# Linear-attention heads feeding a convolution-gated FFN on one core: attention regrouped into one visit per group on four 64x64 tiles, FFN output products one unit late

## The chip, the core and the metric

The kernel runs on one core of one Trainium2 chip. The metric is the device time of one execution in microseconds (us). The kernel before took 343.77 us, the median of three runs (343.47 to 345.69). The changed kernel computes the same thing from the same inputs.

## What is computed

Four batches of eight heads, sequence 768, head width 48. Each head carries a 48x48 state that decays by a vector `w` per step; the output of all heads, 384 wide, goes through a gated FFN of width 1024.

```python
for t in range(S):                       # B=4, H=8, S=768, D=48
    cur = einsum('bhd,bhe->bhde', u * k[t], v[t])
    y[t] = einsum('bhd,bhde->bhe', r[t], state + cur)
    state = w[:, None] * state + einsum('bhd,bhe->bhde', k[t], v[t])
x = y as (B, S, 384)
h = relu(x @ w_in)                       # 384 -> 1024
c = sum_k conv_w[k] * h[t + k - 1]       # 3 taps along the sequence
out = (h * sigmoid(c)) @ w_out           # 1024 -> 384
```

The 768 steps of a batch are cut into six groups of 128 steps, each of two chunks of 64. Inside a chunk the recurrence becomes matrix products: scores (k against r, masked), the diagonal term with `u`, the state's contribution, and the update of the state. `w`'s powers scale k and r beforehand so that the decay is folded in.

## The kernel before

**Order.** Nothing is scheduled at run time. Every piece of work is recorded as an operation with the engines it may run on and a planned cost (`Plan.op`); `Plan.order` then writes one fixed order for each engine, choosing by due times that are counted back from the FFN products, corrected by the table `OFF`. Elementwise products marked "any" go to VectorE (DVE) or GpSimd (POOL), whichever the planner finds better. SyncE (SP) issues every DMA, in one fixed order too. An engine whose next instruction waits holds up everything behind it.

**Attention.** A group's k and r arrive transposed (`KR`, head dimension on the partitions) and token-wise (`KT`), v in `WW`; three buffers of each (`NBUF`). `prep` scales k and r by powers of `w` on DVE (line 351, `KR<-KR,TKR`), moves the scaled r by DMA into the operand tiles `RA` and `RB` (rows 48 wide that share a tile with the masked scores), scales the token-wise k and moves it by DMA into `KTA` and `KTB`, and writes the diagonal into `RA`/`RB` with two selects on POOL (line 566). `scores` is 16 float32 products (lines 581, 582) on two quarters of the array, followed by two masked copies on DVE (line 592). `step` is, for each chunk, 8 products that make the next state (lines 604, 605; the decay is a diagonal block `KTd` beneath k, so 112 or 128 rows deep) and two copies of it on ScalarE (ACT) back into `WW` (line 611), and 8 products that make the output (lines 618, 619). So there are 48 products to a group, in four separate stretches on TensorE (PE). `yout` copies the output to `YY` on ACT (line 628); when two groups are there, six small DMAs `YY<-YY` spread the eighth head pair over the others' free partitions, and then `XT`, the FFN's operand, is written as a high and a low float32r half (line 639 on ACT, line 351).

**FFN.** A unit is a batch's third (batch 0: 254, 256, 258 columns) or half (384 columns); there are nine. For each of a unit's eight blocks of 128 FFN channels, `first` is 9 products into one of two PSUM banks `HP` (line 680), then ReLU on ACT in place (684), middle tap on ACT (685), two taps on DVE (688), sigmoid on ACT (691), the gate product on DVE (692), and the high (ACT, 694) and low half (`GL`, "any", 351). The bank is free only when the gate product has read it. `second` is 9 products of that block into three banks `PO` (line 709), three blocks later (`LAG = 3`). The weights arrive as 64-bit words and are converted on ACT, DVE and "any" (lines 482 to 492). Until the FFN's output products begin, small bf16 products on zeros (line 764) fill gaps of PE.

Of the kernel before, what the change touches and what calls it, by code (L numbers as in the profile page):

```python
# [13 lines left out]

DR = 2
DK = 8
DS = 24
DQ = 6
VIS = 4
SLACK = -8.0  # L20
VWAIT = 0.3
ALONE, AFTER = (), 0
POOLED = ()
LAG = 3
WPRE = 2
LEAD = 6
UP = '3sss'
SPLIT = 2
NW = 12
NT = 3  # L30
T0 = 20
SLOW = 0
TS = 40
DELTA = 0.1
OFF = {
    "ST": -1.69, "f2": -4.55, "T2": 1.29, "X": -1.7, "GL": 0.45, "wi": 5.15, "GG": 11.38, "TT": 4.36,
    "KR": -3.61, "kmv": 0.76, "GH": 0.48, "wo": 1.32, "Rs": -0.21, "av": -1.42, "SG": 3.12, "T1": -2.33,
    "rmv": -12.84, "ymv": -0.78, "wlo": 0.9, "sc": -6.54, "S": 0.59, "ldK": 0.4, "ldT": -0.2, "ldV": -0.95,
    "TK1": -4.02, "TH0": -2.43, "uu": 1.28, "Rz": -2.77, "PW2": -3.54, "o2": 0.26, "cw": -1.69, "KTd": -3.79,
    "psY": -8.17,  # L40
}
PB = 2
ZD = 0
FILL = True
FG = 0
FE = 5000
FN = 256
FW = 3.4
BON = 6
NST = 3  # L50
NBUF = 3

# [9 lines left out]
U = 386  # L62
PAT = {"2": [(0, 382), (382, 386)], "s": [(0, 384), (384, 384)], "3": [(0, 254), (254, 256), (510, 258)]}
UNITS = [(b,) + x for b in range(B) for x in PAT[UP[b]]]
NU = len(UNITS)
WS = 256.0


class Plan:
# [6 lines left out]
    def __init__(self):  # L76
        self.ops = []
        self.last_w, self.last_r = {}, {}
        self.port = []
        self.visits, self.visit, self.rank = {}, {}, {}  # L80

    def op(self, eng, dur, rd, wr, fn, cls="", x=0.0, port=False, visit=None):

# [18 lines left out]
        self.ops.append((dur, x, sorted(pred), fn, cls))  # L105
        self.port.append(port)
        if visit is not None:
            self.visits.setdefault(visit[0], []).append(n)
            self.visit[n], self.rank[n] = visit
        return n  # L110

    def late(self):
# [3 lines left out]
        for i, (dur, x, pred, fn, cls) in enumerate(ops):  # L116
            if "pe" in dur and x:
                late[i] = t
                t += dur["pe"] * (1 + (SLOW if t < TS else 0.0))
# [5 lines left out]
        for i in range(n):  # L125
            late[i] -= OFF.get(ops[i][4], 0.0)
        for m in self.visits.values():
            t = min(late[k] for k in m)
            for k, i in enumerate(sorted(m, key=self.rank.get)):
                late[i] = t + 1e-3 * k  # L130
        return late

    def order(self):
# [3 lines left out]
        left = [0] * n  # L137
        for i in range(n):
            left[i] = len(ops[i][2])
            for j in ops[i][2]:  # L140
                succ[j].append(i)
# [10 lines left out]
        fill, hist = FILL, []  # L152
        lanes = [0.0] * 7
        mode, cur, slack = 0, None, SLACK
        todo_v = {v: set(m) for v, m in self.visits.items()}
        ext = {}
        for v, m in self.visits.items():
            inner = set(m)
            for i in range(n):
                if any(j in inner for j in ops[i][2]) and any(i in ops[k][2] for k in m):  # L160
                    inner.add(i)
            ext[v] = {j for k in m for j in ops[k][2]} - inner
        end_of = [None] * n
        todo = n
        while todo:
            best = None
            for e in self.ENG:
                av = avail[e]
                if not av:
                    continue  # L170
                f = free[e]
                if e == "pe":
                    if cur is not None:
                        av = [i for i in av if self.visit.get(i) == cur]
                    else:
                        c = []
                        for i in av:
# [121 lines left out]
def rwkv_ffn_kernel(tc, krd, krt, vt, wd, ut, w_in, conv_w, w_out, out):  # L299
# [4 lines left out]
    with ExitStack() as ctx:  # L304
# [318 lines left out]
        def yout(g):  # L623
# [6 lines left out]
            if k == 0:  # L630
                return
# [196 lines left out]
```

## Time and profile before

| | |
|---|---|
| timed runs | 343.77 us median (343.47, 343.77, 345.69) |
| span of the profiled execution, first to last instruction | 349.2 us |
| median of the runs against that span | 5.4 us shorter |
| mean granted PE clock | 0.954 |
| busy, of the span | PE 91%, DVE 72%, ACT 62%, POOL 54% |
| bytes moved by DMA | 44.41 MB |

The profile is of one execution; the page gives its span, and no time of its own beyond that. Idle time of an engine is put down to whatever ended it. Records of PE show two for each float32 product (two passes) and one for each float32r product; PEld is the loading of weights, which overlaps.

### The profile page before, as it was taken

How to read it: one execution, taken by the hardware profiler on the slowest of the kernel's cores; microseconds unless marked ns; L12 is line 12 of the kernel's file. 1: busy time of each engine (PE TensorE's matmuls, PEld its weight loads, DVE VectorE, ACT ScalarE, POOL GpSimd, SP SyncE). 2: the span in 40 equal slices, each digit the busy share in tenths (PEclk: the TensorE clock that was granted, in tenths of full speed). 3: DMA queues.
4: the chain of work that ended last, by engine and by line, in shares of the span. 5: the costliest groups of instructions: out<-in, count | busy, mean ns of one | idle time of the engine just before them, and what ended most of it. 6: DMA issues, size and time to landing. Idle time of an engine off the chain costs nothing.

```text
span 349.2 us, 9698 instructions
## 1 busy us (share of the span) xinstructions
PE 319.1 (91%) x3838; PEld 296.3 (85%) x3838; DVE 252.4 (72%) x412; ACT 215.2 (62%) x513; POOL 188.1 (54%) x214
## 2 busy tenths in 40 slices
PE   8899877989998898889869989999899999999995
PEld 4678767879887897879869979999899999999995
DVE  6966868789896788697597797775675655665560
ACT  4516669677756674564547555775575856766751
POOL 8847978688989685956743540232332221242230
PEclk9759989699999999999969999999999999999999
DMA  7958698424564759686624730235420200200101
GB/s 188 266 163 238 211 277 221 156 91 103 172 191 130 219 155 243 168 247 141 191 78 128 188 110 2 79 99 122 128 75 8 75 1 2 79 2 2 68 2 68
DMA packets 25117, 44.41 MB, mean 127 GB/s; under 512 B 5296, under 2 KB 15920, under 8 KB 25072
## 3 DMA queue, kind: packets, MB, share of 16 engines
q1 hardware_dynamic: 25072, 43.79, 45.2%
q8 instruction: 30, 0.49, 0.6%
q14 instruction: 15, 0.12, 0.1%
HBM read 30.40 MB, written 4.72 MB: 101 GB/s over the span
## 4 chain that ended last, share of the span: by engine, by line
PE 52%; DMA 18%; DVE 10%; ACT 8%; POOL 4%; SPq 3%; issue 3%; ACTq 0%; DVEq 0%; POOLq 0%
PE HP L680 22%; PE PO L709 17%; DMA KR<-in_krd_dram 11%; DMA KT<-in_krt_dram 4%; PE psC L581 4%; SPq L354 3%; PE psS L604 3%; PE psY L618 3%; DVE KR L351 2%; DVE CV L688 2%; ACT WW L611 2%; DMA uc<-in_ut_dram 2%; PE PO L764 2%; ACT SG L691 1%; DMA YY<-YY 1%
## 5 line engine op out<-in xcount | busy, mean ns | idle before, releaser
L680 PE MATMUL HP<-XT,wi 128*128 128x386 f32 (+3 forms) x648 | 120.7, 334 | 11.3 <-DVE SG L692 9.7
L680 PEld LDWEIGHTS HP<-XT,wi 128*128 128x128 f32 x648 | 107.1, 197 | 16.4 <-DVE SG L692 13.4
L709 PE MATMUL PO<-GH,wo 128*128 128x384 f32 (+3 forms) x432 | 111.0, 321 | 0.9 <-ACT OS L716 0.9
L688 DVE SCALAR_TENSOR_TENSOR CV<-HP,cw,CV 128x384 f32<-128x384 f32 (+3 forms) x144 | 81.1, 569 | 24.1 <-ACT CV L685 22.6
L351 POOL TENSOR_TENSOR GL<-SG,GH 128x384 fp32r<-128x384 f32 (+3 forms) x49 | 48.5, 990 | 85.4 <-ACT GH L694 71.1
L709 PEld LDWEIGHTS PO<-GH,wo 128*128 128x128 f32 x432 | 76.9, 190 | 1.6 <-ACT OS L716 1.3
L709 PE MATMUL PO<-GL,wo 128*128 128x384 f32 (+3 forms) x216 | 69.6, 322 | 1.2 <-DVE GL L351 1.2
L691 ACT ACTIVATE SG<-CV 128x384 f32<-128x384 f32 (+3 forms) x72 | 35.2, 489 | 36.8 <-DVE CV L688 36.2
L692 DVE TENSOR_TENSOR SG<-HP,SG 128x384 f32<-128x384 f32 (+3 forms) x72 | 36.6, 509 | 23.5 <-ACT SG L691 23.0
L684 ACT ACTIVATE HP<-HP 128x386 f32<-128x386 f32 (+3 forms) x72 | 31.8, 441 | 30.8 <-PE HP L680 30.0
L351 DVE TENSOR_TENSOR KR<-KR,TKR 112x1024 f32<-112x1024 f32 (+1 forms) x26 | 32.8, 1265 | 18.7 <-DMA KR<-in_krd_dram 14.9
L694 ACT CAST GH<-SG 128x384 fp32r<-128x384 f32 (+3 forms) x72 | 34.1, 474 | 18.8 <-DVE SG L692 18.5
L709 PEld LDWEIGHTS PO<-GL,wo 128*128 128x128 f32 x216 | 41.1, 190 | 1.6 <-DVE GL L351 1.4
L685 ACT ACTIVATE CV<-HP,cw 128x384 f32<-128x384 f32 (+3 forms) x72 | 39.2, 545 | 1.6
L611 ACT COPY WW<-psS 48x192 f32<-48x192 f32 x88 | 27.5, 313 | 15.1 <-PE psS L605 13.5
L604 PE MATMUL psS<-WW,KTA 112*48 112x48 f32 x352 | 26.0, 219 | 7.7 <-ACT WW L611 6.0
L604 PEld LDWEIGHTS psS<-WW,KTA 112*48 112x48 f32 x352 | 20.6, 130 | 13.5 <-ACT WW L611 7.1
L566 POOL TENSOR_SCALAR_AFFINE_SELECT RA<-QQ 64x512 f32<-64x512 f32 x24 | 20.3, 848 | 18.2 <-PE psY L619 17.1
L582 PE MATMUL psC<-KR 48*64 48x64 f32 x384 | 29.0, 229 | 0.0
L581 PE MATMUL psC<-KR 48*64 48x64 f32 x384 | 29.0, 229 | 0.0
L618 PE MATMUL psY<-RA,WW 112*48 112x64 f32 x384 | 27.6, 226 | 0.0
L619 PE MATMUL psY<-RB,WW 128*48 128x64 f32 x384 | 27.6, 226 | 0.0
(86 smaller groups left out, 512.3 us busy)
## 6 DMA issues: line engine op xcount, KB each, us to landing
KR<-in_krd_dram SPq DMA_DIRECT2D x24, 448.0 KB, 5.0
KT<-in_krt_dram SPq DMA_DIRECT2D x18, 384.0 KB, 4.3
WW<-in_vt_dram SPq DMA_DIRECT2D x48, 96.0 KB, 3.7
out_dram<-OS SPq DMA_DIRECT2D x18, 192.0 KB, 1.9
ST<-in_w_in_dram SPq DMA_DIRECT2D x8, 384.0 KB, 4.0
ST<-in_w_out_dram SPq DMA_DIRECT2D x8, 384.0 KB, 3.8
RA<-KR SPq DMA_DIRECT2D x22, 96.0 KB, 4.2
RB<-KR SPq DMA_DIRECT2D x22, 96.0 KB, 4.0
```

Source lines behind the costliest of these rows:

```text
L351: op(eng, d, rd, wr, lambda e: e.tensor_tensor(**kw), cls, port=True)
L581: PE.matmul(psC[0:64, n:n + C], kk[64:112, p, t], rr[64:112, p, t], start=True, stop=True)
L604: PE.matmul(psS[64:112, n:n + D], KTA[i][:, p, c, :], WA[i][:, p, c, :], start=True, stop=True)
L611: lambda e, T=T, ps=ps, o=o: A.copy(T[j][o:o + 48, :, cn, :], ps[o:o + 48, 0:NP * D].rearrange("q (p d) -> q p d", p=NP)))
L618: PE.matmul(psY[64:112, n:n + C], WA[i][:, p, c, :], RA[i][0:112, p, t], start=True, stop=True)
L680: PE.matmul(hp, wi[a][:, j, fs], X[:, x, j, t], start=(j == 0 and k == 0), stop=(j == 2 and k == 2))
L685: op("act", act(n) + 0.05, [H_, "cw"], [("T", ti)], lambda e: A.activation(t1, hp[:, 1:n + 1], AF.Copy, scale=cw[:, 3 * f + 1:3 * f + 2]), ...
L688: op("dve", dve(n + 60), [H_, "cw"], [("T", ti)], lambda e, k=k: V.scalar_tensor_tensor(out=t1, in0=hp[:, k:n + k], scalar=cw[:, 3 * f + k ...
L691: op("act", act(n), [("T", ti)], [("SG", ti)], lambda e: A.activation(sg, t1, AF.Sigmoid))
L692: op("dve", dve(n), [H_], [("SG", ti)], lambda e: V.tensor_tensor(out=sg, in0=hp[:, 1:n + 1], in1=sg, op=ALU.mult), "GG")
L694: op("act", act(n), [("SG", ti)], [("GH", gi)], lambda e: A.copy(gh, sg))
L709: PE.matmul(PO[m][:, :n], wo[a][:, f, ms], g2[x], start=(f == 0 and k == 0), stop=(f == NF - 1 and k == 2))
```

## The change

The planner's special rules for visits and the table `OFF` are gone (two entries stay), and its planned costs are other ones; with them, the fixed orders of all engines are new. What is computed in another way:

- `visit(g)` does all products of one step of the loop as one operation on PE: the outputs of group g together with the scores and state updates of group g+1, 64 float32 products, for each chunk and head pair eight of them on the four 64x64 quarters of the array: two scores, two state-times-r, two k-times-v, two outputs.
- The decay of the state is an elementwise product (`M`, any engine), followed by an addition from PSUM on DVE (`SA`). The diagonal blocks `KTd`, the copies of the state on ACT, and the operand tiles `RA`, `RB`, `KTA`, `KTB` are gone with their DMAs.
- The diagonal of the scores is written by an "any" product (`dg`), the mask by one copy of 128 partitions.
- The output goes from PSUM straight into `XT` as high (ACT) and low half (DVE); `XT` has a fourth block for the eighth head pair, which six DMAs a group spread. Before, they were six for two groups.
- `second` of a unit runs beside `first` of the next unit, block of output channels by block of output channels, into a single bank `PO`; there are 13 buffers of gated values instead of five, and four banks `HP` instead of two.
- Units are 254, 256, 258 for batch 0 and 382, 386 for the others; `w_out` is converted in six pieces instead of eight. The zero products end with the first FFN product.

```diff
-        HP = [pst.tile([128, 512], F32, name=f"HP{i}") for i in range(2)]
-        PO = [pst.tile([128, 512], F32, name=f"PO{i}") for i in range(NM)]
+        SP_ = pst.tile([128, NP, 2, C], F32, name="SP")
+        UP = pst.tile([128, 512], F32, name="UP")
+        AV = pst.tile([128, NP, 2, C], F32, name="AV")
+        HP = [pst.tile([128, 512], F32, name=f"HP{i}") for i in range(NH)]
+        PO = pst.tile([128, 512], F32, name="PO")
...
+        def visit(g, av, su):
...
+            def mm(e):
+                for c in range(2):
+                    for p in range(NP):
...
+                        for x in range(2):
+                            if su:
+                                PE.matmul(SP_[xs[x], p, c], KK[j][rows[x], p, t], RR[j][rows[x], p, t], start=True, stop=True)
+                        for x in range(2):
+                            if av and not (first and c == 0):
+                                PE.matmul(outs[x], state(2 * g + c)[rows[x], p], RR[i][rows[x], p, t], start=True, stop=False)
+                        for x in range(2):
+                            if su and not (c == 1 and gj == GPB - 1):
+                                n = (c * NP + p) * D
+                                PE.matmul(UP[rows[x], n:n + D], TOK[j][xs[x], 0, p, c], TOK[j][xs[x], 2, p, c], start=True, stop=True)
+                        for x in range(2):
+                            if av:
+                                PE.matmul(outs[x], TOK[i][xs[x], 2, p, c], SC[g % 2][xs[x], p, c], start=first and c == 0, stop=True)
...
+                op("dve", dve(512, psum=1), ["SUs", "mask"], [("SC", k)], lambda e: V.copy_predicated(
...
+                        tt("any", 192, [ka, "PW2"], [("M", c)], "M", out=m, in0=a, in1=w64, op=ALU.mult)
+                        tt("dve", 192, [("M", c), "SUu"], [kb], "SA", 1, out=b, in0=m, in1=u_, op=ALU.add)
...
+                op("act", act(512), ["AV"], [kh], lambda e: A.copy(xh, y), "XH")
+                tt("dve", 512, ["AV", kh], [kl], "XL", 1, out=xl, in0=y, in1=xh, op=ALU.subtract)
                 for o in (0, 64):
+                    for jx in range(3):
+                        dma([kh, kl], [("Xm", b % 2, gi, o, jx)], X[o + 48:o + 64, :, jx, t].bitcast(F32), X[o + 16 * jx:o + 16 * jx + 16, :, 3, t].bitcast(F32), 0.5, 0.08, "mv")
...
+        for u in range(NU + 1):
+            a, b = need(u), need(u + 1)
+            for f in range(NF):
+                if u:
+                    for k in range(3 * f, 3 * f + 3):
+                        second(u - 1, k)
+                if u < NU:
+                    first(u * NF + f)
```

How the fixed orders stand at three places. **PE, one group in the middle of the program**, before: `psS` takes the state, `psY` the outputs, `psC` the scores, and each stretch is of one kind.

```order
L709 MATMUL PO_126<-GH_97,wo_144 128x384
L604 MATMUL psS<-WW_78,KTA_72 48x48
L605 MATMUL psS<-WW_78,KTB_75 48x48
...
L618 MATMUL psY<-RA_63,WW_78 48x64
L619 MATMUL psY<-RB_66,WW_78 48x64
...
L581 MATMUL psC<-KR_67 64x64
L582 MATMUL psC<-KR_67 64x64
```

PE at such a place now: one visit, of which the first of eight rounds is shown, between FFN products. The four kinds alternate (`SP` scores, `AV` outputs, `UP` updates).

```order
L500 MATMUL HP_127<-XT_77,wi_117 128x258
L442 MATMUL SP<-KR_63 64x64 x2
L445 MATMUL AV<-KR_62,SS_69 48x64 x2
L449 MATMUL UP<-TOK_66 48x48 x2
L452 MATMUL AV<-SC_67,TOK_65 48x64 x2
```

What were 48 products in four stretches are 64 in one, and the visit needs two groups' operands (`KR_63` and `KR_62`) at its first instruction.

**SP, the first issues**, before and now (`ST` takes weights; `KR`, `KT`, `TOK` and `WW` the attention's inputs):

```order
L354 DMA KR_67<-in_krd_dram 112x1024
L354 DMA KR_68<-in_krd_dram 112x1024
L354 DMA KR_69<-in_krd_dram 112x1024
L354 DMA uc<-in_ut_dram 48x4x1 x2
L354 DMA KT_79<-in_krt_dram 128x384
L354 DMA WW_76<-in_vt_dram 64x384 x2
```

```order
L275 DMA TOK_64<-in_krt_dram 128x768
L275 DMA KR_61<-in_krd_dram 48x1024 x2
L275 DMA uu<-in_ut_dram 128x192
L275 DMA TOK_64<-in_vt_dram 64x384 x2
L275 DMA TOK_65<-in_krt_dram 128x768
L275 DMA ST_101<-in_w_in_dram 128x768
```

All of the first group's inputs now come ahead of the second group's, and each group's k and r come in two DMAs.

**PE, late in the program**, now: FFN blocks of one unit (`HP`) stand between output products of the unit before it (`PO`).

```order
L532 MATMUL PO<-GG_87,wo_119 128x382
L500 MATMUL HP_126<-XT_78,wi_116 128x388 x2
L500 MATMUL HP_126<-XT_78,wi_117 128x388
...
L532 MATMUL PO<-GG_88,wo_118 128x382 x2
L532 MATMUL PO<-GG_88,wo_119 128x382
```

Counted along PE's order, the 24th `first` (the last of batch 0) has 50 of the 216 groups of three output products and 9.1 of the 23 units of 64 visit products before it; the 64th has 168 and all 23; 26 groups follow the 72nd.

More of the change, by code (lines that the diff above doesn't have):

```diff
@@ L124, in late @@
                 late[j] = min(late[j], late[i] - m)
[L125 to L131, printed above, removed]
+        return [t - OFF.get(o[4], 0.0) for t, o in zip(late, ops)]
     def order(self):
@@ L151, in order @@
         seq, where, when = [], [None] * n, [None] * n
-        fill, hist = FILL, []
+        fill, hist = True, []
         lanes = [0.0] * 7
[L154 to L163, printed above, removed]
+        mode = 0
         todo = n
@@ L167, in order @@
             for e in self.ENG:
[L168 to L177, printed above, removed]
-                            v = self.visit.get(i)
-                            if v is not None and not (late[i] < slack + f or all(end_of[j] is not None and end_of[j] <= f + VWAIT for j in ext[v])):
-                                continue
-                            c.append(i)
-                        av = c
-                    if not av:
-                        continue
+                av, f = avail[e], free[e]
                 if e == "pool":
@@ L643, in rwkv_ffn_kernel @@
[L643 to L661 removed]
+                        rows = [slice(64 * x, 64 * x + D) for x in range(2)]
@@ L723, in need @@
-            return 3 * (b * GPB + last // GT // 2 * 2 + 2)
-        load(1)
+            return b * GPB + min(t0 + n, S - 1) // GT + 1
         prep(0)
-        scores(0)
-        for g in range(2, NBUF):
+        conv_piece()
+        visit(-1, False, True)
+        for g in range(1, NBUF):
             load(g)
-            prep(g - 1)
-        conv_piece()
-        n0 = need(0)
-        for f in range(WPRE):
-            w_in_piece(f)
-            pieces((f + 1) * n0 // WPRE)
-        pieces(n0)
@@ new lines, in visits @@
+        def visits(n):
+            while done[0] < n:
+                g = done[0]
+                if g + 1 < NG:
+                    prep(g + 1)
+                visit(g, True, g + 1 < NG)
+                if g + NBUF < NG:
+                    load(g + NBUF)
+                done[0] += 1
+        for f in range(2):
+            w_in_piece(f)
+        visits(need(0))
+        for u in range(NU + 1):
[6 more added lines that the diff above has]
+                    first(u * NF + f)
+                if u == 0 and f + 2 < NF:
+                    w_in_piece(f + 2)
+                if u == 0 and f >= 2:
+                    w_out_piece(f - 2)
+                if b > a:
+                    visits(min(b, a + (b - a) * (f + 2) // 7))
```

540 lines of the change are left out of this document (185 added, 355 removed).

## The prediction

> **What bounds the kernel now.** I read the page's shares first, then stages by windows, then who waits on TensorE (PE), then the rows that price the change. Shares, and the stages (busy us of PE, PEld, DVE, ACT, POOL):
>
> ```profile
> span 349.2 us, 9698 instructions
> PE 319.1 (91%) x3838; PEld 296.3 (85%) x3838; DVE 252.4 (72%) x412; ACT 215.2 (62%) x513; POOL 188.1 (54%) x214
> 0.00:140.00 140.00, 123.24 (x1876) 108.17 (x1877) 113.04 (x192) 86.63 (x228) 111.67 (x132) 0.91 0.69 189
> 80.00:100.00 20.00, 19.02 (x294) 17.68 (x294) 18.60 (x34) 13.48 (x36) 18.72 (x20) 1.00 0.61 163
> 140.00:267.00 127.00, 117.22 (x1399) 110.67 (x1400) 94.91 (x147) 77.74 (x176) 55.93 (x63) 0.97 0.45 120
> 300.00:330.00 30.00, 30.00 (x173) 30.00 (x171) 18.49 (x31) 20.95 (x45) 9.75 (x10) 1.00 0.10 36
> L680 PE MATMUL HP<-XT,wi x648: 274/338/687, 42.7 to 335.8; 128*128 128x386 f32 x108, 128*128 128x256 f32 x18, 128*128 128x258 f32 x18, 128*128 128x260 f32 x18
> PE HP L680 <- DVE SG L692: 9.7, 13, 1.6
> PE psS L604 <- ACT WW L611: 6.0, 4, 3.7
> ```
>
> Three stages with three limits. Up to 42.7 us no FFN product runs: inputs and preparation set the pace. Up to about 140 us DVE is busy 81% and POOL 80%, with attention and weight conversion on them. From 300 on PE never rests. PE's named waits are for the gate product (9.7 us, because a bank `HP` is held until then) and for the state's round trip through ACT (6.0).
>
> **PE's part.** An FFN block and a group of attention are priced from the chain and from the order of time in one stretch (start, duration):
>
> ```profile
> 300.23 1.58 PE HP L680 x9
> 301.81 1.57 PE PO L709 x9
> 80.32 2.12 PE PO L709 x18
> 150.75 0.28 PE L709 MATMUL PO<-GH,wo 128*128 128x258 f32 x1
> 150.96 0.24 PE L604 MATMUL psS<-WW,KTA 112*48 112x48 f32 x1
> 151.35 0.22 PE L618 MATMUL psY<-RA,WW 112*48 112x64 f32 x1
> 151.36 0.22 PE L619 MATMUL psY<-RB,WW 128*48 128x64 f32 x1
> 151.41 0.22 PE L618 MATMUL psY<-RA,WW 112*48 112x64 f32 x1
> 152.20 0.22 PE L619 MATMUL psY<-RB,WW 128*48 128x64 f32 x1
> 152.35 0.27 PE L581 MATMUL psC<-KR 48*64 48x64 f32 x1
> 153.28 0.22 PE L582 MATMUL psC<-KR 48*64 48x64 f32 x1
> 153.78 0.21 PE L605 MATMUL psS<-WW,KTB 128*48 128x48 f32 x1
> ```
>
> Nine products of 384 columns take 1.58 us, three 0.525, three of 256 columns 0.35. One group of attention took from 150.87 (0.12 behind the last FFN start) to 153.82: 2.95 us. The two column halves start 10 ns apart (151.35, 151.36) and the next such pass 58 ns later, so two tiles run side by side; a float32 product, which has two records, takes 0.115 us for 64 columns. If four tiles do the same, a visit is 16 rounds of four at 0.115, 1.84 us, and entering and leaving the mode costs the 0.1 us by which 152.35 lies later than a 58 ns step from 152.20, twice: **2.05 us**, 0.9 less a group. If only two run together, 64 products are 32 rounds, 3.7 us; at the closest mean spacing in these rows (16 passes from 150.96 to 151.35, 24 ns each), 128 passes are 3.1. I take 2.05: the rows show tiles that don't wait for each other.
>
> Now PE's sum from the 24th FFN block (the end of batch 0) on: 48 blocks x 1.58 = 75.8; output groups 22 x 0.35 + 144 x 0.525 = 83.3; 13.9 visits x 2.05 = 28.5; together 187.6 us. Before that point PE has only some 63 us of work.
>
> **DVE's part.** Its rows, with the rows that go from other engines:
>
> ```profile
> L688 DVE SCALAR_TENSOR_TENSOR CV<-HP,cw,CV 128x384 f32<-128x384 f32 x96 | 58.7, 616 | 22.3 <-ACT CV L685 20.9
> L688 DVE SCALAR_TENSOR_TENSOR CV<-HP,cw,CV 128x256 f32<-128x256 f32 x16 | 7.5, 476 | 0.7 <-ACT CV L685 0.6
> L692 DVE TENSOR_TENSOR SG<-HP,SG 128x384 f32<-128x384 f32 x48 | 26.6, 554 | 18.4 <-ACT SG L691 18.1
> L692 DVE TENSOR_TENSOR SG<-HP,SG 128x256 f32<-128x256 f32 x8 | 3.3, 416 | 0.7 <-ACT SG L691 0.6
> L351 DVE TENSOR_TENSOR KR<-KR,TKR 112x1024 f32<-112x1024 f32 x22 | 29.6, 1348 | 18.5 <-DMA KR<-in_krd_dram 14.9 <-DMA YY<-YY 2.4 <-issue 1.2
> L592 DVE COPY_PREDICATED RB<-mask,psC 64x512 f32<-64x512 int32 x24 | 17.9, 747 | 0.7
> L351 DVE TENSOR_TENSOR XT<-YY,XT 128x384 fp32r<-128x384 f32 x14 | 11.8, 855 | 1.4 <-ACT XT L639 1.3
> L546 DVE TENSOR_REDUCE QQ<-KT 128x8 f32<-128x384 f32 x18 | 9.8, 544 | 1.2 <-POOL KT L351 1.1
> L486 DVE SCALAR_TENSOR_TENSOR TT<-CC,TT 128x384 int32<-128x384 int32 x16 | 10.6, 668 | 0.0
> L484 DVE TENSOR_SCALAR TT<-ST 128x384 int32<-128x384 int32 x16 | 8.9, 560 | 1.8 <-POOL wi L351 1.7
> L611 ACT COPY WW<-psS 48x192 f32<-48x192 f32 x88 | 27.5, 313 | 15.1 <-PE psS L605 13.5
> L566 POOL TENSOR_SCALAR_AFFINE_SELECT RA<-QQ 64x512 f32<-64x512 f32 x24 | 20.3, 848 | 18.2 <-PE psY L619 17.1
> 154.88 0.54 DVE L546 TENSOR_REDUCE QQ<-KT 128x8 f32<-128x384 f32 x1
> 155.34 1.28 DVE L351 TENSOR_TENSOR GL<-SG,GH 128x384 fp32r<-128x384 f32 x1
> ```
>
> Half of the masked copies go (24 x 0.74 = 17.7 us off). Added, and not in this trace, are 40 additions from PSUM, 192 wide, and 24 subtractions from PSUM, 512 wide. The gate product, which reads PSUM too, costs 0.554 at 384 and 0.416 at 256, 1.08 ns a column: 0.35 and 0.69. The half written into `XT` took 0.855 at 384. I take 0.40 and 0.75 (bounds 0.35 to 0.6, 0.69 to 1.1): 16 + 18 us, of which 11.8 of `XT<-YY` on DVE are replaced. By this DVE has about as much to do as before, 268 us of single durations; those overlap at the hand-over (154.88 + 0.54 ends 0.08 after the next starts), and the union is some 5% less, **255 us against 252.4**. ACT loses 27.5 of state copies; POOL loses two selects a group, but gets the decay product and the diagonal, and stays near 190.
>
> Up to the gate of the 24th block DVE has, by its order and these rows: taps 48 x 0.476 = 22.8, gates 24 x 0.416 = 10.0, scalings of k and r 15.4, ten masks 7.4, ten reductions 5.4, 17 additions 6.8, nine subtractions 6.8, weight conversion 20, set-up, low halves and diagonals 16: 111, as a union **105 us**. At the 81% of 0 to 140 that is 130 us, at the 93% of 80 to 100 it is 113. I take 86%, 122: two more banks `HP` give it three chains to choose from, but the first loads still come first.
>
> **The moves.** The 44 moves into `RA`, `RB` and 32 into `KTA`, `KTB` go, and 72 become 144 for `XT`. On SP, which issues in order, that is about 310 issues instead of 290:
>
> ```profile
> 108.45 0.59 SPq L354
> KR<-in_krd_dram SPq DMA_DIRECT2D x24, 448.0 KB, 5.0
> YY<-YY SPq DMA_DIRECT2D x72, 16.0 KB, 2.7
> 345.63 0.49 ACT OS L716
> ```
>
> At 0.59 us each, 183 us of SP, hidden behind the engines if nothing queues; a block waits for its six moves (2.7 us after the last issue) only in the first unit, since later groups come a unit ahead. The output products a unit late cost PE nothing: the single bank `PO` must be emptied (0.49) before the next eight, and an FFN block or a visit (1.58 or 2.05 us) stands at every such place but the last unit's. They take the gate wait away; if DVE falls behind by more than four banks, the wait is back, which is the second rival. The zero products end with the first FFN product; should the granted clock (0.91 on average up to 140) sink to a half after it, PE's 63 us of work would still just about fit into the 122 that DVE takes.
>
> **The sum.** 122 to the 24th gate; less 4, since its block leaves PE about 4 us earlier (ReLU, tap, two taps, sigmoid, gate); then 187.6 of PE at a rate between 92% (117.22 of 127, with attention) and 100% (300 to 330). DVE must do 150 us in the same time, 75%, as in 140 to 267; in the last units, with attention, nearer 85%. So 93%: 202. Then 3.6 from the last PE product to the end (345.63 to 349.2). 122 - 4 + 202 + 3.6 = 323.6 in the profiled span; the runs' median lies 5.4 under it: **318 us**. With the bounds, 113 - 4 + 188 + 3.6 - 5.4 = 295 and 130 - 4 + 204 + 3.6 - 5.4 = 328.
>
> **The rivals.** *Four tiles don't run together.* Visits of 3.1 to 3.7 us, say 3.5: 13.9 x 1.45 / 0.93 = 22 more, **340**; the visits before the 24th block hide behind DVE. For it: no row shows two row halves and two column halves at once. Against it: the 10 ns between tiles.
>
> The Trainium skill bears on this, and divides. "TensorE: Matmul & The Clock Gate", section "Wait — 56ns, not 53.3ns?", gives a start-to-start floor of about 25 ns however few the columns; by it 128 passes would be an estimated 3.2 us, and this rival holds. Section "Part 3: Packing small matmuls — row/col tiling" of the same page puts only about 4 ns between tiles; by it the visit is 1.84. This trace's 10 ns within a pair agrees with the second, its 24 ns mean with the first.
>
> *DVE sets the pace throughout, and the kernel is slower.* In-order DVE waits for each ACT step of each chain (22.3 and 18.4 us of waits in the rows above), and the visits add two additions and a subtraction to the same queue. To the 64th gate it has 251 us of durations, 237 as a union; PE then has 38 left. At a rate r the time is 237/r + 38 + 3.6 - 4 - 5.4: at the 81% of 0 to 140, 325; at the 75% of 140 to 267, **348**, slower by 1.3%. It is slower than before from a rate below 76%. Against it: in 140 to 267 DVE waited for work that PE was late with, and six gates instead of four can be under way.
>
> *Loads come late.* `KR` and `TOK` are now read until the visit's end, so the load for the group after next but one starts a visit later than before. The loop of two visits has five issues (3.0), landing 5.0, scaling 1.35, k's scaling on POOL 1.1 and the visit 2.05: 12.5 us, against 2 x 10.5 that FFN work gives (a unit's 16 blocks and three visits, 31.4 us, are three steps). It binds only if queueing adds 8.5 us, and then each further us costs some 10.5 in all, half of the 21 visits after the first: **330** at 22 us.
>
> **Chances.** Forecast, PE and DVE sharing the limit, 0.56; DVE at 93% and the time under 300, 0.08; tiles by pairs 0.14; DVE at about 75% 0.14; late loads 0.08. A difference under 1% (340.3 to 347.2 us) can't be told from none here. The first two are faster, 0.64. The tiles' 340 lies on the line: 0.07 faster, 0.07 same. Of DVE's 0.14, 0.10 is slower, 0.02 same, 0.02 faster; of the loads' 0.08, 0.04 faster, 0.02 same, 0.02 slower. Together 0.77 faster, 0.11 same, 0.12 slower. The range, 300 to 345, leaves out 0.08 below and some 0.11 above.
>
> **What would show it.** Right: a round of eight products in a visit about 0.23 us long, the whole near 2 us; the first FFN product by 30 us, not 42.7; the 24th gate near 122; no wait for the gate product on PE after it; the 26 output groups at the end back to back. Wrong: passes of a visit evenly 24 to 29 ns apart (tiles); PE waiting for gate or additions in the last units with DVE above 90% (DVE binds) or DVE itself idle for ACT (rate); `KR` scalings waiting for their DMA as a large group (loads).

## The result and the profile after

| | before | after |
|---|---|---|
| median of the timed runs, us | 344.73 (343.47 to 345.82) | 332.39 (331.53 to 332.88) |
| span of the profiled execution, us | 349.2 | 331.2 |
| end of the 24th FFN gate, us | 146.7 | 129.4 |
| from there to the end, us | 202.5 | 201.8 |
| first FFN product, us | 42.7 | 36.7 |

The ratio is 0.9655, 95% interval 0.9613 to 0.9698: the change gives 12.3 us by the medians, 3.5% by the ratio. Here and below a time is the median of all runs of a kernel, while a ratio leaves out the slow ones, more than 1.5% above the fastest of the same kernel, so the two need not agree exactly. The prediction had 318 us, a gain of 26. The time lies in its range (300 to 345), and the gain is less than half of what it said.

The page's first lines of the changed kernel, and its two stages up to the 24th gate and behind it (start:end, length, then busy us of PE, PEld, DVE, ACT and POOL with their instruction counts, granted clock, DMA share, GB/s):

```profile
span 331.2 us, 10563 instructions
PE 296.4 (90%) x4371; PEld 277.0 (84%) x4371; DVE 265.3 (80%) x439; ACT 168.9 (51%) x380; POOL 185.5 (56%) x201
```

```profile
0.00:129.40 129.40, 103.17 (x1683) 90.23 (x1684) 109.93 (x193) 58.93 (x148) 87.69 (x102) 0.88 0.58 156
129.40:331.20 201.80, 193.26 (x2690) 186.81 (x2688) 155.35 (x247) 110.02 (x232) 97.80 (x99) 0.99 0.33 87
```

Put beside the sum on record: behind the 24th gate 201.8 us (forecast -4 + 202 + 3.6 = 201.6), ahead of it 129.4 (forecast 122). In the profiled span the whole miss, 331.2 against 323.6, lies ahead of the gate.

One visit in the order of time (start, duration), between an FFN block and the next output group, with most of its rows left out:

```profile
196.74 1.73 PE L500 MATMUL HP<-XT,wi 128*128 128x384 f32 x9
198.40 0.27 PE L442 MATMUL SP<-KR 48*64 48x64 f32 x2
198.41 0.26 PE L445 MATMUL AV<-KR,SS 48*48 48x64 f32 x2
...
198.65 0.24 PE L442 MATMUL SP<-KR 48*64 48x64 f32 x2
198.67 0.22 PE L445 MATMUL AV<-KR,SS 48*48 48x64 f32 x2
198.72 0.22 PE L442 MATMUL SP<-KR 48*64 48x64 f32 x2
198.73 0.22 PE L445 MATMUL AV<-KR,SS 48*48 48x64 f32 x2
198.78 0.21 PE L449 MATMUL UP<-TOK 64*48 64x48 f32 x2
198.79 0.22 PE L452 MATMUL AV<-SC,TOK 64*48 64x64 f32 x2
...
200.36 1.34 PE L532 MATMUL PO<-GG,wo 128*128 128x386 f32 x6
```

A block takes 1.59 us (its single cost at this width, as on record: 1.58), so the visit starts at 198.33 and lasts to 200.36: 2.03 us for 128 passes, 16 ns each. Two passes (a row with x2) start together, two others 10 to 20 ns later, and the next four 50 to 70 ns after the first: four tiles at once. The forecast was 2.05.

What PE waits for in the changed kernel, and what DVE's work costs there, grouped by shape (busy us, mean ns of one):

```profile
PE HP L500 <- DVE SG L513: 10.2, 6, 3.0
PE HP L500 <- DMA XT<-XT: 3.9, 2, 2.5
```

```profile
L272 DVE TENSOR_TENSOR KR<-KR,TKR 112x1024 f32<-112x1024 f32 x22 | 41.4, 1882 | 0.0
L272 DVE TENSOR_TENSOR XT<-AV,XT 112x512 fp32r<-112x512 f32 x24 | 16.3, 679 | 3.2 <-ACT XT L479 3.2
L272 DVE TENSOR_TENSOR SS<-MM,UP 112x192 f32<-112x192 f32 x40 | 13.7, 343 | 4.2 <-PE UP L449 2.1 <-POOL GG L272 1.4 <-POOL MM L272 0.4
L370 DVE SCALAR_TENSOR_TENSOR TT<-CC,TT 128x512 int32<-128x512 int32 x6 | 8.2, 1360 | 0.0
```

The additions (0.343) and subtractions (0.679) from PSUM came in at or under the prices on record (0.40, 0.75). What became dearer is work that the change didn't touch: the scaling of k and r, 1.348 before and 1.882 now.

### The profile page after: what moved, and what is told of

It reads as the page before. It is cut to its first block, busy times and chain, and to the rows that moved or that the text cites. A ratio compares the mean times of both kernels' runs of the same rounds, so it can differ in the third digit from the quotient of the medians.

```text
span 331.2 us, 10563 instructions
## 1 busy us (share of the span) xinstructions
PE 296.4 (90%) x4371; PEld 277.0 (84%) x4371; DVE 265.3 (80%) x439; ACT 168.9 (51%) x380; POOL 185.5 (56%) x201
## 4 chain that ended last, share of the span: by engine, by line
PE 50%; DVE 20%; DMA 10%; issue 6%; POOL 6%; ACT 5%; SPq 2%; DVEq 0%; ACTq 0%; POOLq 0%
PE HP L500 20%; PE PO L532 19%; DMA ST<-in_w_out_dram 6%; DVE CV L509 4%; DVE KR L272 3%; PE SP L442 3%; PE HP L532 3%; POOL TOK L272 2%; DVE GG L272 2%; PE AV L452 2%; POOL GG L272 2%; SPq L275 2%; PE AV L445 2%; DMA TOK<-in_krt_dram 2%; DVE TT L370 1%
## 5 line engine op out<-in xcount | busy, mean ns | idle before, releaser
L500 PE MATMUL HP<-XT,wi 128*128 128x384 f32 (+4 forms) x648 | 123.3, 339 | 15.6 <-DVE SG L513 10.2
L532 PE MATMUL PO<-GG,wo 128*128 128x382 f32 (+4 forms) x600 | 110.7, 327 | 8.6 <-POOL GG L272 2.9
L532 PEld LDWEIGHTS PO<-GG,wo 128*128 128x128 f32 x600 | 97.7, 194 | 12.3 <-POOL GG L272 3.7
L509 DVE SCALAR_TENSOR_TENSOR CV<-HP,cw,CV 128x382 f32<-128x382 f32 (+4 forms) x144 | 77.2, 565 | 12.5 <-ACT CV L506 11.9
L272 POOL TENSOR_TENSOR GG<-SG,GG 128x382 fp32r<-128x382 f32 (+4 forms) x48 | 49.6, 1044 | 32.6 <-ACT GG L515 29.9
L442 PE MATMUL SP<-KR 48*64 48x64 f32 x768 | 46.7, 233 | 0.8 <-DVE SC L457 0.4
L452 PE MATMUL AV<-SC,TOK 64*48 64x64 f32 x768 | 47.1, 222 | 0.0
L272 POOL TENSOR_TENSOR TOK<-TOK 128x384 f32<-128x384 f32 x23 | 24.4, 1062 | 37.4 <-DMA TOK<-in_krt_dram 36.7
L445 PE MATMUL AV<-KR,SS 48*48 48x64 f32 x704 | 44.2, 223 | 0.4 <-DVE XT L272 0.2
L442 PEld LDWEIGHTS SP<-KR 48*64 48x64 f32 x768 | 39.2, 138 | 6.0 <-issue 2.2
L449 PE MATMUL UP<-TOK 64*48 64x48 f32 x704 | 41.2, 209 | 1.2 <-DVE SS L272 1.2
```

What stands on the lines that cost most here:

```text
L272: op(eng, d, rd, wr, lambda e: e.tensor_tensor(**kw), cls, port=not psum)
L442: PE.matmul(SP_[xs[x], p, c], KK[j][rows[x], p, t], RR[j][rows[x], p, t], start=True, stop=True)
L445: PE.matmul(outs[x], state(2 * g + c)[rows[x], p], RR[i][rows[x], p, t], start=True, stop=False)
L449: PE.matmul(UP[rows[x], n:n + D], TOK[j][xs[x], 0, p, c], TOK[j][xs[x], 2, p, c], start=True, stop=True)
L452: PE.matmul(outs[x], TOK[i][xs[x], 2, p, c], SC[g % 2][xs[x], p, c], start=first and c == 0, stop=True)
L500: PE.matmul(hp, wi[a][:, j, fs], X[:, x, j, t], start=(j == 0 and k == 0), stop=(j == 2 and k == 2))
```

## The experiments

Gate means the end of the 24th FFN gate in the profiled execution, rest the time from there to the end of its span; each is of a single execution. In the traces of the kernels that differ in the order of the tiles or in what issues the transfers (moves thrice among them), and in that with zeros until the first output product, DVE and POOL run their instructions in the changed kernel's order. In all the others the planner also wrote new orders, which is a second difference. The kernel before ran beside each set of kernels, at 344.1 to 345.6 us. In short, with the expectations and readings below:

| run | us | ratio to before [95%] | gate | rest |
|---|---|---|---|---|
| changed kernel | 332.39 | 0.9655 [0.9613, 0.9698] | 129.4 | 201.8 |
| two tiles at a time | 345.25 | 1.0038 [0.9986, 1.0089] | 131.2 | 212.5 |
| two banks `HP` | 343.06 | 0.9931 [0.9864, 0.9997] | 138.6 | 202.6 |
| not a unit late | 345.60 | 1.011 [0.9907, 1.0313] | 123.8 | 217.7 |
| zeros until first output product | 331.17 | 0.9654 [0.9559, 0.975] | 128.4 | 199.4 |
| zeros for 24 blocks | 334.1 | 0.9791 [0.966, 0.9921] | 136.3 | 196.1 |
| no token scaling | 321.84 | 0.9328 [0.9255, 0.9402] | 123.8 | 196.1 |
| no low bits | 326.17 | 0.9458 [0.9408, 0.9508] | 129.4 | 197.0 |
| low halves on POOL | 331.59 | 0.9626 [0.957, 0.9682] | 130.8 | 198.5 |
| zeros and low halves | 332.80 | 0.9789 [0.9575, 1.0003] | 129.8 | 200.8 |
| third staging tile | 339.75 | 0.9845 [0.9789, 0.99] | 127.0 | 209.3 |
| first moves on ACT | 334.03 | 0.9634 [0.9544, 0.9724] | | |
| 72 moves on ACT | 326.13 | 0.9428 [0.9367, 0.9489] | 130.5 | 194.6 |
| third moves thrice | 354.34 | 1.0229 [1.0136, 1.0322] | 150.7 | 203.9 |
| 66 later moves on ACT | 321.97 | 0.938 [0.9329, 0.9431] | 125.6 | 196.0 |
| stores on ACT | 329.75 | 0.9537 [0.9435, 0.9638] | 128.6 | 199.9 |
| 66 moves and stores on ACT | 323.88 | 0.9425 [0.9374, 0.9476] | 127.2 | 195.4 |
| before, 66 moves on ACT | 340.14 | 0.9841 [0.9797, 0.9884] | | |

### The kernel before, again

No edit.

> The kernel before, profiled a second time and changed in nothing. The forecast took the 5.4 us by which its profiled span lay over the median of its runs as something that every kernel would have. If that is so, the span is again near 349 us with a time near 344. If the first profile was a long execution by chance (its granted clock was 0.67 and 0.65 between 10 and 30 us), the span comes out near 343 to 346, and the first 43 us are shorter.

Its span was 344.6 us in a run that took 346.4, and the 24th gate stood at 146.0. The 349.2 us of the first profile were a long execution. By the second profile the change gave 13.4 us of span: 16.6 ahead of the gate, and 3.2 lost behind it, where 198.6 became 201.8.

### Four tiles at once: two at a time

```
-for c in range(2):
-    for p in range(NP):
-        ... SP (2 products), AV from the state (2), UP (2), AV from SC (2)
+for half in range(2):
+    for c in range(2):
+        for p in range(NP):
+            ... half 0: SP (2), UP (2);  half 1: AV from the state (2), AV from SC (2)
```

> The same 64 products of a visit in another order: first all scores and updates, which use only two of the four quarters, then all state products and outputs, which use the other two. The fixed orders of the engines stay as they are. If four tiles run side by side in the changed kernel, a visit grows from about 2.0 us to 3.5 (32 rounds of two, of which eight are 48 columns), 1.5 more; 13.9 visits after the 24th gate make 21 us, and those before it hide behind DVE partly: 350 to 357 us. If visits gained nothing from four tiles, the time stays at 332.

The same visit here:

```profile
199.59 1.73 PE L503 MATMUL HP<-XT,wi 128*128 128x384 f32 x9
201.25 0.33 PE L444 MATMUL SP<-KR 48*64 48x64 f32 x4
...
203.10 0.28 PE L452 MATMUL AV<-KR,SS 48*48 48x64 f32 x4
...
204.78 1.34 PE L535 MATMUL PO<-GG,wo 128*128 128x386 f32 x6
```

From 199.59 + 1.59 to 204.78 it takes 3.6 us instead of 2.03. Four tiles are what makes the visit short, and the order of the products decides whether they get there. The time is 345.25, 12.9 us more and no better than before; the 22 of the rival on record were not reached, since PE's idle time behind the gate (8.5 us in the changed kernel, 212.5 - 208.9 = 3.6 here) took part of it up.

### Two banks, and the output products not late

`NH = 4` becomes `NH = 2`; and, by itself, the output products of a unit behind its own FFN blocks:

```
 for f in range(NF):
-    if u:
-        for k in range(3 * f, 3 * f + 3):
-            second(u - 1, k)
     if u < NU:
         first(u * NF + f)
...
+for k in range(3 * NF if u < NU else 0):
+    second(u, k)
```

> The changed kernel with two banks for the FFN blocks, as before the change, instead of four. If the extra banks are what keeps PE from waiting for the gate product, PE waits for it again at many of the 72 blocks, some 0.5 to 1 us each: 350 to 375 us. If lateness of the second products alone removes the wait, or DVE sets the pace whatever the banks, the time stays within 3 us of 332.

> The output products of a unit are written behind that unit's own eight blocks instead of beside the next unit's; four banks and 13 buffers of gated values stay. If the lateness is what keeps PE from waiting, PE and DVE now work in bursts: for each of six units of 384 columns PE waits some 4 us for the last gates and then DVE idles through part of 12.6 us of output products: 345 to 365 us. If the four banks alone do it, the time stays within 4 us of 332.

With two banks 343.06 us (337.9 to 345.9 over ten runs), with the products on time 345.60. The waits of PE, first with two banks, then with products on time:

```profile
PE HP L500 <- DVE SG L513: 17.2, 12, 2.5
```

```profile
PE PO L532 <- POOL GG L272: 10.2, 18, 1.7
```

The two banks bring PE's wait for the gate product back, and the gate is 9.2 us later. Products on time wait for the low half of a value that has just been made, 18 times. Their gate is earlier (123.8), because less output work stands ahead of it, and the rest is 15.9 longer. Each of tiles, banks and lateness, undone alone, costs 10.7 to 13.2 us by the medians, 2.8 to 4.6% of the time before by the ratios: most or all of the gain each time. They don't add up; in these runs each is needed for the others to pay. For banks and lateness the orders are new as well, so some of that may be the orders'.

### Ahead of the gate: clock, DVE, POOL, staging

The zero products run to the first output product instead of the first FFN product (`cls != "f1"` becomes `"f2"`); and small zero products of 128 columns are put in until the 24th FFN block, into the unused columns of the updates' bank.

> The zero products go on until the first output product of the FFN instead of ending with its first block. Theory: up to the 24th gate DVE's work sets the pace, and the clock granted to PE there (0.76 to 0.91 between 40 and 140 us) costs nothing: within 2 us of 332. Rival: the early stage is long because PE runs slowly between blocks; then the clock between 36 and 60 us rises and the time falls by 3 to 6 us.

> The zero products (128 columns each, into an unused stretch of the bank of the updates) fill PE's planned gaps until the 24th FFN block is under way, instead of ending with the first block. In the changed kernel PE was busy 103 of the first 129 us at a mean granted clock of 0.88, though the products there need only some 63 us at full clock. Theory A, the clock stretches that stage: it rises above 0.95 and the 24th gate comes 4 to 9 us earlier, time 323 to 328. Theory B, that stage waits for a mixture of loads, moves and DVE, and PE's slower products fit into those waits: the gate moves by less than 2 us.

Both came out near the changed kernel (331.2, 334.1). In the second the clock from 60 us to the gate rose to 0.96 to 1.00 (0.88 to 0.95 in the changed kernel), but the gate was 7 us later, because the zeros had waits of their own:

```profile
PE UP L586 <- DVE SS L273: 7.1, 3, 3.8
```

The clock isn't what holds the stage up, as far as these two can tell.

Then DVE's work. Three lines of the preparation go in one kernel (the token-major products and scalings of k and r, `KRT`, `KS` and `KRU`); in the other the two instructions that put together the low three bits of a converted weight become one shift.

> The three products per group on the token-wise k and r are left out (scaling of k, and the two that make the diagonal from r, k and u; 70 of 72 stand on POOL), so the state and the diagonal are of unscaled numbers. All DVE work but two products stays. Theory: DVE's products of two SBUF operands ran long (scaling of k and r 1.88 us in the changed kernel, priced at 1.35) because POOL's products run beside them; without 70 of POOL's, the scaling falls to 1.2 to 1.4, DVE's busy time by 12 us or more, and the 24th gate comes by 122. Rival: DMA traffic or the width makes them long; then they stay at 1.7 to 1.9.

> The weight conversion leaves out the lowest three bits of each mantissa, so one DVE instruction of two goes in each of 15 pieces, some 12 us of DVE's work, all of it ahead of the 24th gate; ACT, POOL and the loads stay. Theory: DVE's work sets the pace of that stage; at its rate of 86% the gate comes 10 to 14 us earlier, and the time is 319 to 324. Rival: loads or the chain of ACT steps set the pace; then less than 4 us are won.

The stage up to the gate, first without token scaling, then without low bits:

```profile
0.00:123.80 123.80, 94.60 (x1672) 85.02 (x1673) 91.38 (x188) 60.16 (x150) 53.56 (x72) 0.91 0.63 166
```

```profile
0.00:129.40 129.40, 98.49 (x1697) 87.86 (x1697) 97.32 (x183) 60.34 (x150) 80.93 (x97) 0.91 0.60 158
```

DVE is relieved of 18.6 and 12.6 us ahead of the gate, and the gate moves by 5.6 and by nothing, where the theory said 10 to 14 for the second. So the gate doesn't follow DVE's work at a fixed rate; that theory falls. The times did move, by 10.6 and 6.2 us: without low bits that is more than the 4 of the rival, and in the profiles the whole difference, 4.8 us, lies behind the gate. Since both kernels also have new orders, what the 6.2 us come from stays open. What both show at PE, more than the changed kernel with its 3.9 us, is a wait for a transfer, the move of rows inside `XT`, again first without token scaling, then without low bits:

```profile
PE HP L497 <- DMA XT<-XT: 12.6, 3, 5.5
```

```profile
PE HP L498 <- DMA XT<-XT: 12.0, 3, 6.3
```

The kernel without token scaling, where POOL has less to do, also showed that POOL lengthens some of DVE's instructions; the groups are in the last section.

Three more, with a small result: the low halves of the gated values on POOL alone (`tt("any", ...)` becomes `tt("pool", ...)`), the same with the longer zeros, and a third staging tile (`NST` 2 to 3, with `NGB` 13 to 11 to make room, so that some gated values are overwritten before their last products).

> All 72 subtractions of the gated values' low half on POOL; the planner had put 24 of them on DVE, where they took 22 us (1.1 us each at 386 columns). POOL gets 24 us more, 210 in all. Theory: DVE is the engine short of time in both stages, so the time falls by 4 to 12 us. Rival: POOL becomes the late one for the output products, or its longer work stretches DVE's; then the time stays or grows.

> Zero products until the first output product, and all low halves of the gated values on POOL; each alone came out about 1 us below the changed kernel. If they add up, 329 to 331 us. If both relieve the same wait, 331 to 332.

> Three staging buffers for the weights instead of two (as before the change), paid for with 11 instead of 13 buffers of gated values. Theory (DVE's work sets the early stage): the 24th gate moves by less than 3 us. Rival: the chain's stretches on weight loads (three of 6 to 7 us between 40 and 80 us) are what the stage waits for; then it comes 5 to 10 us earlier.

331.59, 332.80 and 339.75 us. The gate moved by +1.4, +0.4 and -2.4. Eleven buffers cost the third kernel its time behind the gate; at its gate staging was worth 2.4 us at most.

### SP's queue

After that nothing on an engine was left that had moved the gate much. SP issues all transfers in its order, and the prediction had costed its 310 issues at nothing. Two kernels split the moves inside `XT`, with the order on PE, DVE and POOL row for row the same:

```
-def dma(rd, wr, dst, src, dur=0.5, x=0.1, cls=""):
-    op("sp", dur, rd, wr, lambda e: SP.dma_start(dst, src), cls, x)
+def dma(rd, wr, dst, src, dur=0.5, x=0.1, cls="", q=SP):
+    op("sp", dur, rd, wr, lambda e: q.dma_start(dst, src), cls, x)
...
-    dma(..., 0.5, 0.08, "mv")
+    dma(..., 0.5, 0.08, "mv", A if o else SP)
```

The first of them has `A if g < 3 and o else SP`. A third kernel issues the moves of the third group three times over, on SP.

> Of the 18 moves inside XT that the first three groups need, the nine of the upper rows are issued by ACT instead of SP; the order of PE, DVE and POOL is the same row for row. Start theory: from the first FFN product to the 24th gate it took 92.7 us in the changed kernel, 90 to 93 in six variants and by my forecast (30 and 122) 92, so that most of the 7.4 us missing at the gate were lost before the first product (36.7 us instead of 30), on the chain third visit, XT on ACT and DVE, six moves on SP with two loads among them. Three of the six on ACT save about 2 us of SP's issues (0.59 each): first product at 34 to 35, 24th gate at 127 to 128, about 330 us. Rival, something in the 93 us after the first product sets the gate: first product earlier, gate at 129 to 130, 332 us.

> The moves of the upper rows are issued by ACT for all 24 groups, 72 of the 144. Start theory: the same 2 us as with the first three groups alone, and besides it ACT has 72 more issues of about 0.6 us, 43 us, in its order ahead of ReLUs and sigmoids: DVE's waits for ACT grow and the time is 330 to 340 us. Rival, the moves' queue on SP sets the pace of stage A (PE waited 12 us for XT moves when DVE was relieved): 24th gate before 126 and below 328 us.

> The six moves of the third group are issued three times each, twelve more issues on SP at 0.59 us, 7 us; nothing else is changed, and the values are the same. Start theory: first product at 43 to 44 us, 24th gate 6 to 7 us later, at about 136, and 338 to 339 us in all. Rival, the 93 us after the first product have slack that takes the delay up: gate at 130 to 132, 332 to 334 us.

The start theory falls. With 72 moves on ACT the first blocks came later, since ACT has the moves behind weight conversions there, and yet the gate is only 1.1 us later and the time 6.3 less:

```profile
34.94 0.59 PE L500 MATMUL HP<-XT,wi 128*128 128x256 f32 x3 [1.55 <-DMA XT<-XT]
41.28 5.02 PE L500 MATMUL HP<-XT,wi 128*128 128x256 f32 x24 [5.75 <-DMA TOK<-in_vt_dram]
```

With the first three groups alone the first blocks were as late (40.9) and nothing was won: 334.03 us. (Its profile is of a run of 337.72 us, so no gate is given.)

The third kernel did another thing than was meant, and told more by it. The first unit needs only two groups, so the third group's moves belong to the second unit. And a repeated move waited for the one ahead of it to land. SP's rows in the changed kernel, and with the moves thrice:

```profile
50.65 3.86 SPq L275 DMA_DIRECT2D XT<-XT  x6
55.44 0.38 SPq L275 DMA_DIRECT2D ST<-in_w_out_dram  x1
```

```profile
50.70 27.51 SPq L275 DMA_DIRECT2D XT<-XT  x18
78.31 0.53 SPq L275 DMA_DIRECT2D ST<-in_w_out_dram  x1
```

SP was held 23.65 us longer, the weights behind it were issued 22.9 us later, the gate came 21.3 us later and the end 22.0. How the delay reached PE stands in the rows of ACT and PE of this run. ACT waited for those weights with the copies of gated values behind them in its order, and PE's next output product waited for such a copy:

```profile
82.82 0.66 ACT L366 ACTIVATE CC<-ST 128x512 f32<-128x512 f32 x1 [24.23 <-DMA ST<-in_w_out_dram]
84.12 0.58 PE L532 MATMUL PO<-GG,wo 128*128 128x254 f32 x1 [21.54 <-ACT GG L515]
```

So at this place SP's queue has some 2.4 us of slack (23.65 against 21.3), no more: moves, loads and weights are in one line, and the line is nearly critical. The second unit's own rows came late too, though (its first block started at 87.97 us instead of 65.38); had they been the only late ones, the gate would have come later as well, and the run doesn't tell by how much.

A load that comes right behind the moves can be seen in the changed kernel itself, behind the gate:

```profile
139.33 4.32 SPq L275 DMA_DIRECT2D XT<-XT  x6
143.75 0.53 SPq L275 DMA_DIRECT2D TOK<-in_krt_dram  x1
149.36 1.01 POOL L272 TENSOR_TENSOR TOK<-TOK 128x384 f32<-128x384 f32 x1 [3.91 <-DMA TOK<-in_krt_dram]
```

The chain of work that ended last passes through this load (5.54 us) and from there, over POOL, ACT and DVE, to a block of PE at 160.09. Whether its buffer would have been free before 143.75 isn't shown.

### The relief without the late start

`A if g > 1 and o else SP` leaves the first unit's moves on SP. Beside it, the output stores issued by ACT, with the moves left on SP, and both together.

> As the run with 72 moves on ACT, but the moves of the first two groups, which the first FFN unit needs, stay on SP, since there ACT had them behind weight conversions (27 products of the first three blocks came at 41.3 us instead of 36.7). Queue theory: SP, which issues in order, was within 2.5 us of setting the pace when the second unit's moves were due (23.8 us more there moved the 24th gate by 21.3), and its relief was partly given back at the start. Then the first product is at 36 to 37, the 24th gate at 126 to 128, and the time 322 to 325 us. Rival, SP's queue matters only after the gate (PE's idle time there fell from 8.5 to 4.2 us): gate 129 to 131, 325 to 328 us.

> The output stores are issued by ACT, which wrote the values, instead of SP; the moves stay on SP. SP waited 46 us in all, 8 times, for the output values, with loads and moves behind. Queue theory, any issue that holds SP costs: 24th gate little changed (few stores before it), PE's idle time after it from 8.5 to about 4 us, 326 to 329 us. Rival, only the moves' own issues count, since the planner puts the stores late: 331 to 333 us.

> Both: the upper moves from the third group on and the stores go to ACT. Queue theory: whichever of the two is better, and up to 3 us below it, 320 to 325 us, with PE idle under 4 us after the gate. Rival, ACT with some 90 more issues in its order becomes late itself: DVE's waits for ACT (30.6 us for sigmoid and tap in the changed kernel) above 40, and 328 to 335 us.

The first gives 321.97 us, 10.4 less than the changed kernel, and is the fastest version that computes all of the reference. Its stages, and its moves by issuing engine (KB each, median us to landing):

```profile
0.00:125.60 125.60, 97.42 (x1683) 85.18 (x1684) 108.51 (x193) 59.92 (x148) 88.07 (x104) 0.91 0.63 164
125.60:321.60 196.00, 192.50 (x2689) 187.01 (x2688) 148.27 (x248) 111.18 (x232) 97.25 (x98) 0.99 0.33 88
```

```profile
XT<-XT SPq DMA_DIRECT2D x78, 16.0 KB, 2.5
XT<-XT ACTq DMA_DIRECT2D x66, 16.0 KB, 2.4
```

The gate is 3.8 us earlier, the rest 5.8 shorter, with PE idle for 196.0 - 192.5 = 3.5 us in it instead of 8.5; of PE's waits behind the gate (3.0 us for a gate product, 1.9 for copies of the output) none is left. DVE still does 108.5 us of work ahead of the gate (109.9 without the relief). A move doesn't land sooner (2.4 and 2.5 us, 2.2 in the changed kernel): it is issued sooner, and so is what stood behind it. Nothing but the issuing engine differs here, so the 10.4 us are the relief's. Not all of them need be the queue's directly, since the new timing also changed what meets what on DVE and POOL (two scalings of k and r behind the gate took 4.47 us each in the changed kernel, here the longest takes 2.05). A rest of 196 to 197 us also stands in the table for three kernels with every issue on SP, though with new orders. The stores alone give 2.6 us, with runs from 325.8 to 331.6, which can't be told from nothing; with the moves they give back 1.9 (323.88).

The Trainium skill has this in "DMA: Bandwidth & Descriptors", section "Issuing engines are not separate DMA queues": issuing from several engines saves only the time that a sequencer needs to start a transfer, usually little beside the transfer itself. The landing times agree with the first half; here the little that is saved, 66 x 0.59 us of SP's time, was worth 10 us.

### The same relief in the kernel before

66 of the 72 moves of its outputs go from SP to ACT, in the same way.

> The kernel before, with 66 of the 72 moves inside its outputs (all but those of the first two groups) issued by ACT instead of SP, as many as in the changed kernel at 322.0 us. If SP's queue is something that the change made worse (it puts six moves a group where three stood, due just before a unit), the kernel before gains little: 340 to 344 us, or loses, since its ACT is busier (62% of the span). If the queue held both kernels back alike, it gains the same 10 us, 333 to 336 us, and the shortfall of the change's gain isn't the queue's.

340.14 us, between the two expectations: its ratio of 0.9841 is 5.4 us. With the relief in both kernels the change is worth 340.1 - 322.0 = 18 us instead of 12.3 (4.6% by the ratios instead of 3.5). So about half of the 10.4 us looks like a price that the kernel before paid too, and half like what the change added to the queue; the moves of the two kernels stand at different places, so the split is rough.

## Why the prediction was right and wrong

**Right.** The visit: 2.03 us, forecast 2.05, by four tiles at once; undoing that gave 3.6 us, the 3.7 on record for two. Of the two sections of the Trainium skill that the prediction weighed ("TensorE: Matmul & The Clock Gate"), the one on packing came nearer: 2.03 us was measured, where it made 1.84 and the other 3.2, and 16 ns a pass is under the floor of about 25 ns that the other gives. Behind the gate 201.8 us, forecast 201.6, but that is luck, since two errors cancel: 193.3 us of PE instead of 187.6, at 96% instead of 93%. The three parts that the sum rests on (tiles, banks, lateness) are each worth 10.7 to 13.2 us when undone. DVE had 265 us of work rather than 255 (the scalings of k and r alone took 41.4 instead of 29.6), but did it at the rate forecast, 85% ahead of the gate and 77% behind it (86% and 75%).

**Wrong: the term of SP.** "At 0.59 us each, 183 us of SP, hidden behind the engines if nothing queues" is the step that failed. The sum of issues was right, and so was the condition, but it was then costed at nothing. SP's order mixes moves that wait for a visit with loads and weights that don't, and each group has six moves due just before a unit, where the kernel before had three (and some 76 others, tied to loads and weights of attention). Taking 66 of them off SP brought the span from 331.2 to 321.6, beside the 323.6 of the sum on record. That the two lie so close is partly luck: the sum was short only ahead of the gate, by 7.4 us, and the relief gave 3.8 there and 5.8 behind it. The prediction did see a queue in its rival of late loads, at 330 us, but gave it 0.08 because it counted one loop of loads and not the moves among them. The rival in which DVE sets the pace throughout didn't come: PE was 96% busy behind the gate, though from 247 to 267 us DVE was busy all of the 20 us and PE 18.8.

**Wrong: the reason for the 122.** That term was DVE's 105 us of work at 86%. DVE had 109.9 us at 85%, which gives 129.4, and this looked like a term that was only mis-sized. It isn't only that: 12.6 us less of DVE's work (in new orders) left the gate where it was, while the relieved queue brought it to 125.6 with nearly the same work in the same order. DVE's share looks like an outcome more than a limit. Of the 7.4 us, 3.8 went with the relief of the queue; the other 3.6 stay open. Without token scaling, which relieves DVE and POOL together, the gate came to 123.8, but that leaves work out.

**Wrong: the correction by the run.** The sum was made in the profiled span and 5.4 us were taken off, because the one profile of before lay that much above the median. A second profile of before lay 1.8 us under its own run's time, and that of the changed kernel 1.2 under its median; wherever a run is on record with its span, its time is 1.7 to 2.1 us above the span. Some 6.6 of the 14 us by which the forecast missed come from reading one long execution as a constant.

**Its own tests.** First product by 30 us: 36.7, and 24th gate near 122: 129.4, both wrong, and both ahead of the gate where the miss lies. Output groups back to back, visit near 2 us: right. No wait of PE for the gate product behind the 24th gate: one of 3.0 us is left, where the kernel before had 2.5 us in five; ahead of it there are 7.2 us more.

## What to carry over

An engine that only issues transfers is an in-order queue like the others: lay its order out in time, with what each issue waits for, before its cost is called hidden. To test it, delay one entry or issue some entries from another engine with every other order unchanged; that told more here than seven kernels that relieved busy engines, the clock and the staging, since six of the seven also got new orders. And a busy share at the forecast rate doesn't show that the engine sets the pace: take some of its work away, with the orders kept if possible, and see how far each stage moves.

## What the runs showed of the hardware

Some of DVE's instructions get longer when POOL works beside them, those with two operands in SBUF above all, and more than had been priced. The groups without token scaling, where POOL has 115 us of work in all instead of 185, beside those of the changed kernel above:

```profile
L272 DVE TENSOR_TENSOR KR<-KR,TKR 112x1024 f32<-112x1024 f32 x22 | 29.6, 1346 | 3.7 <-DMA KR<-in_krd_dram 3.7
L272 DVE TENSOR_TENSOR XT<-AV,XT 112x512 fp32r<-112x512 f32 x24 | 16.4, 685 | 6.2 <-ACT XT L476 5.9
L370 DVE SCALAR_TENSOR_TENSOR TT<-CC,TT 128x512 int32<-128x512 int32 x6 | 4.8, 793 | 0.0
```

The scaling of k and r falls from 1.882 to 1.346 us and the weights' bits from 1.360 to 0.793, while the subtraction that reads PSUM stays (0.679 and 0.685). The Trainium skill, "SBUF — State Buffer", section "SBUF: two separate sides", has DVE instructions with two SBUF inputs and POOL's that read SBUF take turns on a shared pair of ports, each holding it for a whole instruction. The rows above agree with that. But two inputs aren't the whole of it: the shift of the weights' bits on line 368, with one input in SBUF, also falls, from 0.988 to 0.506 us at 512 columns. Nor is it the amount of POOL's work: the kernel before had 188 us of it, and its scaling took 1.348. It depends on what meets what. One scaling of the changed kernel, with the first and the last of four products on POOL:

```profile
132.83 4.47 DVE L272 TENSOR_TENSOR KR<-KR,TKR 112x1024 f32<-112x1024 f32 x1
132.59 0.69 POOL L272 TENSOR_TENSOR MM<-SS,PW 112x192 f32<-112x192 f32 x1
...
135.20 1.02 POOL L272 TENSOR_TENSOR TOK<-TOK,uu 128x384 f32<-128x384 f32 x1
```

It begins after the first of them, the four follow each other until 136.22, and it ends 1.08 us after the last, about what the shortest scaling takes (1.21). So here POOL went four times in a row while DVE stood. The chain of work that ended last passes through this scaling and one more of 4.47 us; what that cost in the end isn't shown apart.

Four tiles of 48 to 64 rows and columns run at once in float32, at 16 ns a pass on average over a visit, where two at a time took 28 ns (3.6 us for 128 passes).
